# Single-block slot sums, VectorE log stores throughout, a first output chunk in halves, and a new order, in a one-core attention and soft-MoE kernel

## The chip, the cores and the metric

The kernel runs on one core of a Trainium2 chip, in float32. TensorE multiplies matrices into PSUM, VectorE (DVE), ScalarE (ACT) and GpSimd (POOL) do the rest, and SyncE (SP) issues the loads of the large tensors and every store. The metric is device time in microseconds of a whole execution. The kernel before was timed three times, and one more execution was profiled; all times below are from that execution, counted from the start of its span.

## The reference

Two stages follow each other. The first is an attention with 32 inducing points, the second a soft mixture of experts on its output. The names `q` and `c` below are used in this text again.

```python
def mab(q, kv):                       # twice: h = mab(I, x), then y = mab(x, h)
    s = scale * (q @ kv.T); s = s - s.max(-1)
    a = exp(s); a /= a.sum(-1) + 1e-9
    return a @ kv
logits = y @ phi                      # 45824 tokens, 32 slots
d = softmax over the tokens of logits # one maximum and one sum for each slot
slot_input = d.T @ y
slot_out = relu(slot_input @ w1[e]) @ w2[e]   # 8 experts, 4 slots each, F = 1024
c = softmax over the slots of logits
out = c @ slot_out
```

x is 4 batches of 11456 rows by 128. The slots' softmax runs over all tokens, so no row of the output exists before every row of x has been read and the experts are done.

## The kernel before, in words

**Chunks.** A batch is six chunks of 15 blocks of 128 rows, 24 chunks in all; a chunk is 128 x 1920 numbers, 960 KB. x is loaded as rows (`xn`) and, for chunks 6 to 23, a second time transposed (`xt`); TensorE transposes the first six.

**First pass** (for each batch). `s1p` = inducing points by x, maxima, exponentials, and `ha` = their product with x (L408); from the batch's sums come `hs`, `hts` and `bdg`.

**Second pass** (for each chunk). `s2p` = x by h (L332), a DVE transpose to `bt` (L579), maximum (L582), subtraction on POOL (L586), exponential on ACT, a TensorE transpose `tt` (L595), the product `lp` with `bdg` (L608), which gives logits and row sums at once, and the store of the logits into `l_all`. DVE stores them for 23 chunks (`ble`, L627, with the last block by ACT in `blf`); for chunk 17 (`BA`) ACT stores all 15 blocks one by one (`bla`, L648) and adds the logarithm's shift, so that POOL need not scale `bt` for it (`bml`, L652).

**Segments.** Three chunks make a segment, eight in all. Its slot maxima (`h0` or `blm`, `pt`, `pb`) are subtracted from the logits (`ds`, L727, on POOL or DVE), ACT takes the exponential (`de`, L730), and TensorE adds up the slot sums `u` (`c2`). For segments 3 to 6 (`C2P`) `c2` takes two blocks at a time: 64 x 64 products at L739, of which the halves on the diagonal are wanted, and four copies of 32 x 32 fetch them (L756). For the other four segments it takes one block at a time: fifteen 32 x 32 products at L745, and one copy (L758). A float32 product leaves two records in the trace.

**Experts.** `sit` joins the slot sums; `hpm` is the first layer (64 products for each of two halves, L902), `ga` the ReLU on ACT, `htm` a transpose, `gc` a DVE copy into `z2`, `so` the second layer (L931), `sos` its copy, `sr` the spread of it over all partitions (L941), and `srs` = `sr` times the reciprocal `rz` of the slots' sum (L944).

**Third pass and output.** The softmax over the slots (`soft`, L514 to L550, `ml` on POOL at L997, and a transpose back into `l_all` at L1000) can run for any chunk whose logits are there. Once `srs` exists, `po` (L1025) makes four products of 480 columns for each chunk, ACT and DVE copy them to `ot` (L1036), and SP stores `ot` (L1044). `SPLIT` gives how many of the four groups go in one store: chunk 1, which is stored first, goes in four stores.

**Order.** Nothing is scheduled at run time: `op` collects steps, and the string `ORDER` (two characters a step) says in which order they are written out. Each engine executes its own steps in that order, and waits with semaphores. PSUM has eight banks, taken in turn (`mm`). `fill` steps (L238) are products of 128 x 128 into a bank of their own that nothing reads; their operand is the tile that also holds `srs`, which is zero until L944 writes it.

Of the kernel before, what the change touches and what calls it, by code (L numbers as in the profile page):

```python
# [43 lines left out]
BA = [17]  # L44
C2P = [3, 4, 5, 6]
# [9 lines left out]
ORDER = (  # L55
    "000102030e0p0A0L0W3v3z0406080a0507090b0c0f0l0h0j0g0i0k0m0q0u0s0w0n0r0t0v0x0B0F0y0d0D0C0E0G0H0M0O0N0o0z17180P0S191a1f1g0Q1i1j0X11130Z0Y0I0R0T1012141l1h1k0J0U150K0V161b1c3D3H3L3P3w3A"
    "1d1m1e1o1phV1n3E1r1s1x1y1u1q1t1z3x3B1B1v3I1C1w3M3F1D3J1A3N1E1F1G1H3Q3R3S3T1K1X1L3U3V3W4b3Z4842451I2C2P2a1Y1M1Z3X401N1O202b211J2c3u3y3C3G3K3O683Y41321P434e2D2Q2E332R464f222d2e2f1Q23"
    "1R241S2F2S252g2T1T344g1U264447491V2G274ccj2h3536282i2H2j2k4a4d1W2Icr2l2n2J4h4icz2U29ck2mcscA4j2Kcl2L2o2p2M5f2q4n5s4k2Vct2rcBcmcucCcn2Nco2s2v2ycv2t2wcDcH4o4A6c6g6k6o6s676b6f6j6n6r8K"
    "4N694B4p4C6d2u2xcp4q4D2z2A4O6a6e5g4PcE5tcF5h37382W4l394r2X4s3a5i2Y4m2Z3bcq3c303d4t5j5u4Q2O5v4E4R5w2BcIcJ3f6h6p6l5F6i6t3g4u3h3i3j4v3k3n4F6m6q6u5G6v6w4wcw4S4G4T3l5k4H5l4I5H4zcx5I6x6y"
    "3m6z6C4U5x5y4V4xcKcP6A5m6D6B6E5J6F4J4W6I4X4K6G6J4Y4L4y5K6OcL6L3e4Z3q315z506R6H6K6McycQ6S51cX6P5L5McG5n5A525o5B6T3o5pcY4M5E5N5OcM5C6N6Q8L6UcR6V6W535D6X545P5Q3r5q70d5cS3p7d5556587q3s"  # L60
    "575b8M717e727f7r7S7T5S7s7U8O8S8W90948J8N8R8V8Z938T8i8P8Q737gcN8X5991855a8U8Y92745c5R7t7h7u5d7V7W5ecO956Y756Z5T7i7v763t7jcTcZ7796975U98997X787w5V7k7x868j9a878k799b9ed65r887l9h7y5W89"
    "8l9c9f7m9d9g7a7z7n7A7Y7p5X609k7o7b8a9i9lcUcV7B8b637Z9j9m7D8m9n809q9o9t8c8n7E9u5Y64d78o8d619r9p9sdd81cW7F8e9vd08fdl9w7c7Cde8h845Z7G9x8p8gd17H9y7I82df9z8q7J8r8s8t9E9S62a67K65ayd87LaM"
    "7M7N9Fdg9G9T9Ua7aza8aAaNaO9H7O9Vd99I7P839Wdhb07Qa966aa9J9A9X9KaBaC9YaPb19Bb2ab9LaQ9Macbrbsbtbubvbwbxbybz8u9Ndi9Ob3bB9Za0b4aD8v9PaEa18wa29Rad8xaRaFb5ae8ya3aSafaga5ahaj9Qa4aTaGaHbCaI"
# [86 lines left out]
def tile_kernel(ctx, tc, x0, xn, xt_d, ind_t, phi, w12, w3, consts, out):  # L150
# [417 lines left out]
    def second(n):  # L568
# [592 lines left out]
```

## Time and profile before

| | us |
|---|---|
| three timed executions | 217.75, 219.30, 220.89 |
| their median | 219.30 |
| the profiled execution, whole | 219.41 |
| span of its profile | 217.4 |
| TensorE busy | 193.3 (89%) |
| DVE, ACT, POOL busy | 163.3, 141.9, 124.4 |
| read and written | 49.84 MB and 23.59 MB |

The span is what lies between the first and the last instruction of the trace; 2.0 us of the profiled execution lie around it. Busy shares are means over very different stages, so a stage is read by the rows of its own stretch: which engine has no gap there, and what the last wait ends on.

### The profile page before, as it was taken

How to read it: one execution, taken by the hardware profiler on the slowest of the kernel's cores; microseconds unless marked ns; L12 is line 12 of the kernel's file. 1: busy time of each engine (PE TensorE's matmuls, PEld its weight loads, DVE VectorE, ACT ScalarE, POOL GpSimd, SP SyncE). 2: the span in 40 equal slices, each digit the busy share in tenths (PEclk: the TensorE clock that was granted, in tenths of full speed). 3: DMA queues.
4: the chain of work that ended last, by engine and by line, in shares of the span. 5: the costliest groups of instructions: out<-in, count | busy, mean ns of one | idle time of the engine just before them, and what ended most of it. 6: DMA issues, size and time to landing. Idle time of an engine off the chain costs nothing.

```text
span 217.4 us, 6563 instructions
## 1 busy us (share of the span) xinstructions
PE 193.3 (89%) x2614; PEld 131.8 (61%) x2614; DVE 163.3 (75%) x371; ACT 141.9 (65%) x395; POOL 124.4 (57%) x137
## 2 busy tenths in 40 slices
PE   7889999999989999999999999999999799775510
PEld 7559674597365897469985698798554345232200
DVE  0114576999999999999987899777968888856240
ACT  2578442975637994449979798724489998936030
POOL 0000000588986968986976699799846686570300
PEclk9999999999999999999999999999999996755585
DMA  6999999998899999999999930000099999999995
GB/s 217 383 425 417 413 417 413 417 417 325 259 397 418 424 414 414 403 414 417 416 417 413 420 154 3 2 8 3 19 400 415 404 427 411 427 410 425 413 392 206
DMA packets 12414, 73.86 MB, mean 340 GB/s; under 512 B 1632, under 2 KB 2272, under 8 KB 12384
## 3 DMA queue, kind: packets, MB, share of 16 engines
q1 hardware_dynamic: 11952, 73.27, 83.3%
q8 instruction: 21, 0.34, 0.6%
q10 hardware_dynamic: 432, 0.17, 0.3%
q14 instruction: 9, 0.07, 0.1%
HBM read 49.84 MB, written 23.59 MB: 338 GB/s over the span
## 4 chain that ended last, share of the span: by engine, by line
PE 70%; DVE 12%; DMA 4%; ACT 4%; issue 2%; POOL 2%; SPq 1%; POOLq 0%; DVEq 0%; ACTq 0%
PE po L1025 12%; PE ha L408 10%; PE s2p L332 9%; PE s1p L332 9%; PE lp L608 8%; PE tt L595 5%; DMA xn<-xn 4%; PE u L739 4%; PE tp L309 3%; DVE ot L1036 2%; DVE l_all L1000 2%; POOL ct L997 2%; PE so L931 2%; PE fill L238 2%; DVE cm L514 2%
## 5 line engine op out<-in xcount | busy, mean ns | idle before, releaser
L1025 PE MATMUL po<-l_all,srs 32*128 32x480 f32 x192 | 41.2, 744 | 9.1 <-DVE l_all L1000 8.5
L1036 ACT COPY ot<-po 128x480 f32<-128x480 f32 x65 | 32.8, 583 | 10.9 <-PE po L1025 10.9
L1025 PEld LDWEIGHTS po<-l_all,srs 32*128 32x128 f32 x192 | 18.8, 219 | 29.5 <-issue 12.3
L586 POOL TENSOR_TENSOR bt<-bt,bm 128x480 f32<-128x480 f32 x24 | 23.6, 995 | 13.8 <-DVE bm L582 12.1
L997 POOL TENSOR_TENSOR ct<-ct,cz 128x480 f32<-128x480 f32 x24 | 23.6, 995 | 13.4 <-DVE cz L550 13.4
L608 PE MATMUL lp<-bdg,a2t 128*128 128x132 f32 x192 | 25.4, 277 | 0.7 <-issue 0.7
L343 DVE TENSOR_SCALAR_CACHE_REDUCE s<-s1p 128x480 f32<-128x480 f32 (+1 forms) x24 | 15.0, 646 | 14.2 <-PE s1p L332 13.9
L727 POOL TENSOR_TENSOR d<-l_all,m_all 128x512 f32<-128x512 f32 x19 | 21.8, 1166 | 6.5 <-issue 3.5
L608 PEld LDWEIGHTS lp<-bdg,a2t 128*128 128x128 f32 x192 | 23.3, 190 | 1.6 <-issue 1.3
L1036 DVE COPY ot<-po 128x480 f32<-128x480 f32 x31 | 18.9, 638 | 6.2 <-PE po L1025 6.1
L652 POOL TENSOR_TENSOR bt<-bt,bz 128x480 f32<-128x480 f32 x23 | 22.6, 997 | 0.3 <-DVE cz L550 0.3
L523 POOL TENSOR_TENSOR ct<-l_all,cm 128x512 f32<-128x512 f32 x18 | 18.8, 1051 | 5.8 <-DVE l_all L1000 5.3
L389 ACT ACTIVATE s<-s,negm 128x480 f32<-128x480 f32 (+1 forms) x24 | 16.6, 694 | 6.2 <-DVE negm L374 6.2
L332 PE MATMUL s1p<-xt,it_sb 128*32 128x480 f32 x160 | 19.3, 570 | 0.7 <-ACT xt L317 0.7
L1000 DVE STREAM_TRANSPOSE l_all<-ct 128x480 f32<-128x480 f32 x24 | 15.6, 659 | 5.0 <-POOL ct L997 5.0
L408 PE MATMUL ha<-xn,e 128*32 128x128 f32 x570 | 19.0, 275 | 0.0
L332 PE MATMUL s2p<-xt,hts 128*32 128x480 f32 x160 | 18.9, 571 | 0.0
L345 POOL MEMSET s<- 128x16 f32 x4 | 0.4, 112 | 31.1 <-DVE e L392 30.8
L527 ACT ACTIVATE ct<-ct 128x480 f32<-128x480 f32 x24 | 14.6, 616 | 5.0 <-POOL ct L523 4.7
L589 ACT ACTIVATE bt<-bt 128x480 f32<-128x480 f32 x24 | 14.1, 610 | 4.9 <-POOL bt L586 4.8
L579 DVE STREAM_TRANSPOSE bt<-s2p 128x480 f32<-128x480 f32 x24 | 15.6, 665 | 2.1 <-PE s2p L332 1.1
L408 PEld LDWEIGHTS ha<-xn,e 128*32 128x32 f32 x570 | 16.1, 109 | 1.6 <-PE s2p L332 0.6
(142 smaller groups left out, 390.5 us busy)
## 6 DMA issues: line engine op xcount, KB each, us to landing
out<-ot SPq DMA_DIRECT2D x20, 960.0 KB, 7.9
xn<-xn SPq DMA_DIRECT2D x18, 960.0 KB, 12.6
xt<-xt SPq DMA_DIRECT2D x14, 960.0 KB, 14.7
w<-w SPq DMA_DIRECT2D x8, 960.0 KB, 14.8
l_all<-xn SPq DMA_DIRECT2D x5, 960.0 KB, 10.1
l_all<-xt SPq DMA_DIRECT2D x4, 960.0 KB, 6.8
out<-ot SPq DMA_DIRECT2D x6, 480.0 KB, 5.0
out<-ot SPq DMA_DIRECT2D x4, 240.0 KB, 2.3
```

The costliest lines, as they stand in the source:

```text
L332: nc.tensor.matmul(dst[32 * g : 32 * g + 32, :w], lhs, src, start=True, stop=True)
L389: nc.scalar.activation(t[:, :v], t[:, :v], AF.Exp, bias=T["negm", b, g], accum_out=z6[:, a : a + 1])
L408: nc.tensor.matmul(ha[32 * q : 32 * q + 32, :P], T["e1", a][:, j * S : (j + 1) * S], T["xn", a][:, j * P : (j + 1) * P], start=c == lo and ...
L523: nc.gpsimd.tensor_tensor(t.rearrange("p (a e s) -> p a e s", s=S, e=2), l_blocks(n), m, op=ALU.subtract)
L586: nc.gpsimd.tensor_tensor(t, t, T["bm", n][:, :nb].unsqueeze(2).broadcast_to(full), op=ALU.subtract)
L608: nc.tensor.matmul(pt[:, q * 4 * SZ : (q * 4 + m) * SZ], t[: m * S, q * P : (q + 1) * P], bdgs[b % 2].rearrange("p q s -> p (q s)")[: m * ...
L652: nc.gpsimd.tensor_tensor(t, t, T["bz", n][:, :nb].unsqueeze(2).broadcast_to(full), op=ALU.mult)
L727: e.tensor_tensor(t.rearrange(o, s=S, e=2), l_pairs(n), m, op=ALU.subtract)
L997: nc.gpsimd.tensor_tensor(t, t, T["cz", n][:, :nb].unsqueeze(2).broadcast_to([P, nb, S]), op=ALU.mult)
L1000: nc.vector.transpose(l_of(n), T[ck][:, :w])
L1025: nc.tensor.matmul(ptile("mm", ("po", 4 * n + g))[:, :w], T["srs",][q, :], l_of(n)[q, :], start=True, stop=True)
L1036: (nc.vector.tensor_copy if dve else nc.scalar.copy)(ot[:, g * w : (g + 1) * w], T["po", m][:, :w])
```

## The change

The change takes `BA` and `C2P` out, with the code that they switched on: all 24 chunks have their logits stored by `ble` and `blf` and their `bt` scaled by `bml`, and all eight segments sum their slots one block at a time, with one copy each. Without the logarithm the early load of ACT's function table goes too. In the experts `rz` is now applied by DVE in `ge`, on the way from `so` to `sos`, and `gs` becomes an ACT copy. Chunk 1 (`HEAD`) gets its four output products in halves of 240 columns, DVE and ACT copying two groups each, and is stored in four stores of other shapes. The `fill` steps go from 16 to 10. Costs in `op` calls are used by nothing at run time. `ORDER` is new throughout.

```diff
-BA = [17]
-C2P = [3, 4, 5, 6]
-SPLIT = {0: 4, 1: 1, 2: 4, 3: 2, 22: 2, 23: 4, 10: 2, 21: 4, 5: 4}
+SPLIT = {0: 4, 2: 4, 3: 2, 22: 2, 23: 4, 10: 2, 21: 4, 5: 4}
+HEAD = 1
-NF = 16
+NF = 10
 ORDER = (
-    "000102030e0p0A0L0W3v3z0406080a0507090b0c0f0l0h0j0g0i0k0m0q0u0s0w0n0r0t0v0x0B0F0y0d0D0C0E0G0H0M0O0N0o0z17180P0S191a1f1g0Q1i1j0X11130Z0Y0I0R0T1012141l1h1k0J0U150K0V161b1c3D3H3L3P3w3A"
...
+    "000102030e0p0A0L0W3v3z3D0406080507090a0b0c0f0l0h0j0g0i0k0m0q0w0u0s0n0r0t0v0x0B0D0y0d0o0z17180F0M0H0Q190C0E0N0G0O0S1a1f1i0P0I1g1j0X0Z13110Y100R0T12141l1h1k0J0U153H3L3P3u3y3A3w0K0V16"
...
-    if BA:
-        nc.scalar.preload_act_table_set("natural_log_exp_and_others")
...
-        if n in BA:
-            op("ACT", 0.2 + (0.17 if valid(n) < w else 0), ("bln", n), bln, [("bz", n)], [("bl", n)])
-            op("ACT", 0.1 + 0.19 * nb, ("bla", n), bla, [("lp", n), ("bz", n), ("bl", n), *need], [("l", n), ("lx", n), *first], [(x[0], x) for x in first])
-        else:
...
-                for j in [0, 2, *range(nb - 1, 3, -2 * nb), *range(4, nb - 1, 2)] if k in C2P else ():
-                    r, h = min(2, nb - j), 64 * (j // 2 % 2)
-                    nc.tensor.matmul(
-                        u[h : h + r * S, : r * S], a2[:, j * S : (j + r) * S], d[:, j // 2, :r], start=i == 0 and j < 4, stop=i == seg - 1 and nb - 6 < j < nb - 1,
-                    )
-                for j in range(nb) if k not in C2P else ():
+                for j in range(nb):
                     q = slice(32 * (j % 4), 32 * (j % 4) + 32)
                     c = slice(j * S, j * S + S)
                     nc.tensor.matmul(u[q, :S], a2[:, c], d[:, j // 2, j % 2], start=i == 0 and j < 4, stop=i == seg - 1 and j >= nb - 4)
...
-                for q in range(4) if k in C2P else ():
-                    r = slice(32 * q, 32 * q + 32)
-                    nc.scalar.copy(us_all[r, k * S : (k + 1) * S], T["u", k][r, q % 2 * S : (q % 2 + 1) * S])
-                if k not in C2P:
-                    nc.scalar.copy(us_all[:, k * S : (k + 1) * S], T["u", k][:, :S])
+                nc.scalar.copy(us_all[:, k * S : (k + 1) * S], T["u", k][:, :S])
...
         def ge():
-            nc.vector.tensor_copy(stile("h", ("sos",), P, 1), T["so",][:, :P])
+            nc.vector.tensor_scalar_mul(stile("h", ("sos",), P, 1), T["so",][:, :P], T["rz", "l"])
...
         def gs():
-            nc.vector.tensor_scalar_mul(T["srs",], T["sr",][:, :P], T["rz", "l"])
+            nc.scalar.copy(T["srs",], T["sr",][:, :P])
...
+        cuts = [0, w // 2, w] if n == HEAD else [0, w]
+        parts = list(zip(cuts, cuts[1:]))
...
+                    nc.tensor.matmul(ptile("mm", ("po", n, g, h))[:, : hi - lo], T["srs",][q, :], l_of(n)[q, lo:hi], start=True, stop=True)
...
+                if n == HEAD:
+                    dve = g % 2 == 1
...
+        todo = [(0, 1, 0, w // 2), (1, 3, 0, w // 2), (3, 4, 0, w), (0, 3, w // 2, w)] if n == HEAD else [(g, g + step, 0, w) for g in range(0, 4, step)]
```

The order moves work at many places; three bear on what follows. All three are TensorE's.

The first is the end of the second pass, where the last segment's maxima go through `pt` and `pb`. `u_2268` (before) and `u_2313` (after) are the sums of segment 6, `hb` and `ufp` small products for the experts. Before:

```order
L238 MATMUL fill_2256<-srs 128x128
L696 MATMUL pt_2258<-cst,tm_2198 32x128 x3
L739 MATMUL u_2268<-d_2246,bt_1978 64x64 x2
L739 MATMUL u_2268<-d_2246,bt_1978 32x32
L739 MATMUL u_2268<-d_2246,bt_1978 64x64 x5
L703 MATMUL pb_2277<-cst,mc_2265 128x32
L739 MATMUL u_2268<-d_2248,bt_1984 64x64 x2
L739 MATMUL u_2268<-d_2248,bt_1984 32x32
L739 MATMUL u_2268<-d_2248,bt_1984 64x64 x5
```

And with the change:

```order
L235 MATMUL fill_2299<-srs 128x128
L675 MATMUL pt_2301<-cst,tm_2219 32x128 x3
L719 MATMUL u_2313<-d_2281,bt_1939 32x32 x15
L479 MATMUL hb_2329<-hs_1858,cst 128x128
L682 MATMUL pb_2331<-cst,mc_2311 128x32
L719 MATMUL u_2313<-d_2283,bt_1954 32x32 x15
```

Between `pt` and `pb` stood eight products of a pair sum; now fifteen single ones and `hb`, which came earlier before.

The second is the turn from the experts' first layer (`hpm`) to the second (`so`). Before:

```order
L902 MATMUL hpm_2453<-w_2077,ma 32x128 x8
L902 MATMUL hpm_2453<-w_2079,ma 32x128 x2
L915 MATMUL htm_2488<-cst,ma 128x128
L238 MATMUL fill_2496<-srs 128x128
L915 MATMUL htm_2498<-cst,ma 128x128
L931 MATMUL so<-w_2079,ma 32x128 x6
```

And with the change:

```order
L872 MATMUL hpm_2517<-w_2084,ma 32x128 x2
L885 MATMUL htm_2543<-cst,ma 128x128
L856 MATMUL zpp<-ones,vr 128x1
L872 MATMUL hpm_2517<-w_2084,ma 32x128 x6
L872 MATMUL hpm_2517<-w_2086,ma 32x128 x2
L901 MATMUL so<-w_2086,ma 32x128 x6
L901 MATMUL so<-w_2088,ma 32x128 x7
L901 MATMUL so<-w_2090,ma 32x128 x8
L901 MATMUL so<-w_2092,ma 32x128 x3
L885 MATMUL htm_2593<-cst,ma 128x128
L901 MATMUL so<-w_2092,ma 32x128 x4
```

The first half's transpose now stands inside the second half of `hpm`, and the second half's transpose inside the first half of `so`.

The third is the end of the experts and the first output products. Before:

```order
L931 MATMUL so<-w_2087,mb 32x128 x4
L886 MATMUL zpp<-ones,vr 128x1
L238 MATMUL fill_2593<-srs 128x128
L941 MATMUL sr<-sos,cst 128x128
L238 MATMUL fill_2598<-srs 128x128
L238 MATMUL fill_2600<-srs 128x128
L1025 MATMUL po_2603<-l_all,srs 128x480
```

And with the change:

```order
L901 MATMUL so<-w_2094,mb 32x128 x4
L911 MATMUL sr<-sos,cst 128x128
L1000 MATMUL po_0_0_2662<-l_all,srs 128x240
L1000 MATMUL po_1_0_2664<-l_all,srs 128x240
L1000 MATMUL po_2_0_2666<-l_all,srs 128x240
L1000 MATMUL po_3_0_2668<-l_all,srs 128x240
L1000 MATMUL po_0_1_2674<-l_all,srs 128x240
```

`zpp` has moved ahead, the three fills are gone, and so are five more that stood between the second and the third chunk's `po`. The two fills right ahead of `hpm` stay, and eight stand earlier.

## Rows read from the trace of the kernel before

**Rows 1.** Windows: stretch, length, busy PE, PEld, DVE, ACT, POOL, clock, DMA share, GB/s.

```profile
110.00:126.00 16.00, 16.00 (x210) 10.44 (x202) 13.12 (x25) 13.19 (x45) 10.66 (x11) 1.00 1.01 414
126.00:131.00 5.00, 5.00 (x46) 4.85 (x45) 4.91 (x13) 4.76 (x18) 5.00 (x6) 1.00 0.24 95
131.00:144.00 13.00, 12.83 (x235) 10.91 (x234) 10.35 (x28) 9.37 (x33) 11.27 (x14) 1.00 0.01 3
...
160.00:175.00 15.00, 13.73 (x79) 6.29 (x72) 13.04 (x27) 14.79 (x35) 9.63 (x11) 1.00 1.02 412
...
190.00:205.00 15.00, 8.44 (x32) 4.33 (x36) 8.05 (x17) 5.77 (x13) 6.59 (x8) 0.50 1.01 418
```

**Rows 2.** Timeline of SP, the first and the last stores: start us, us, operation.

```profile
156.50 0.82 SPq L1044 DMA_DIRECT2D out<-ot  x2
...
208.60 0.33 SPq L1044 DMA_DIRECT2D out<-ot  x1
...
210.62 0.42 SPq L1044 DMA_DIRECT2D out<-ot  x1
```

**Rows 3.** The chain that ended last: start us, us, engine, tile, line, records.

```profile
110.87 0.94 PE u L739 x16
...
136.93 1.01 PE u L739 x16
...
141.95 0.82 PE u L745 x60
...
153.68 0.36 DVE srs L944
154.08 0.71 PE fill L238 x4
154.79 1.82 PE po L1025 x16
156.62 2.25 PE fill L238 x10
...
203.66 3.67 PE po L1025 x16
```

**Rows 4.** Timeline of DVE, 118 to 153 us: idle time ahead in brackets, with what ended it.

```profile
118.05 0.68 DVE L579 STREAM_TRANSPOSE bt<-s2p 128x480 f32<-128x480 f32 x1 [0.51 <-PE u L739]
119.81 0.68 DVE L579 STREAM_TRANSPOSE bt<-s2p 128x480 f32<-128x480 f32 x1 [1.08 <-PE s2p L332]
...
152.82 0.28 DVE L938 COPY sos<-so 128x128 f32<-128x128 f32 x1
```

**Rows 5.** Timeline of ACT, four places.

```profile
4.16 0.29 ACT L230 COPY bdg<-cst 128x4 f32<-128x4 f32 x2 [2.14 <-DMA cst<-consts]
...
114.59 4.16 ACT L648 ACTIVATE l_all<-lp,bl,bz 128x32 f32<-128x32 f32 x15
...
140.04 0.74 ACT L756 COPY us_all<-u 32x32 f32<-32x32 f32 x4 [0.17 <-PE u L739]
...
155.91 2.87 ACT L1036 COPY ot<-po 128x480 f32<-128x480 f32 x6 [1.74 <-PE po L1025]
```

**Rows 6.** Timeline of PE, the experts' two layers.

```profile
144.01 3.70 PE L902 MATMUL hpm<-w,ma 128*32 128x128 f32 x128
...
148.88 1.95 PE L931 MATMUL so<-w,ma 128*32 128x128 f32 x64 [0.45 <-DVE ma L920]
150.66 1.93 PE L931 MATMUL so<-w,mb 128*32 128x128 f32 x64
```

**Rows 7.** Groups by line and form over the span: count, busy us, mean ns, idle before.

```profile
L1036 ACT COPY ot<-po 128x480 f32<-128x480 f32 x65 | 32.8, 583 | 10.9 <-PE po L1025 10.9
...
L652 POOL TENSOR_TENSOR bt<-bt,bz 128x480 f32<-128x480 f32 x23 | 22.6, 997 | 0.3 <-DVE cz L550 0.3
...
L627 DVE TENSOR_TENSOR l_all<-lp,bz 128x448 f32<-128x448 f32 x23 | 13.6, 604 | 0.3
...
L473 ACT COPY ht<-htp 128x128 f32<-128x128 f32 x4 | 1.1, 263 | 0.0
```

More of the change, by code (lines that the diff above doesn't have):

```diff
@@ L69 @@
+    "hFfjfqhGhwfrfshyfefthEhvhjhdhAhzfkflhxfuhnfvhHhIhMhohJhKfmfnhLhOhVhZhNhWhPhShXhQhYhRi0hUhphBhT"
 )
@@ L1019, in output @@
         w = width(n)
-        def mm():
-            btile("x", ("ot", n))
-            for g in range(4):
-                q = slice(32 * g, 32 * g + 32)
-                nc.tensor.matmul(ptile("mm", ("po", 4 * n + g))[:, :w], T["srs",][q, :], l_of(n)[q, :], start=True, stop=True)
-        po = [("po", 4 * n + g) for g in range(4)]
-        i = op("PE", 1.0, ("po", n), mm, [("srs",), ("l", n)], po, [("mm", k) for k in po] + [("x", ("ot", n))], ni=16)
-        plan.uses(("ot", n), i)
-        for g in range(4):
-            m = 4 * n + g
-            dve = g == 2 and n in OD or g == 1 and n in OD2
-            def ev(m=m, g=g, dve=dve):
-                ot = T["ot", n]
-                (nc.vector.tensor_copy if dve else nc.scalar.copy)(ot[:, g * w : (g + 1) * w], T["po", m][:, :w])
-            i = op("DVE" if dve else "ACT", dv(w) if dve else ac(w), ("oe", n, g), ev, [("po", m)], [("otg", m)])
-            plan.uses(("ot", n), i)
@@ L1041, in st, with mm, ev @@
-        def st(lo, hi):
+        cuts = [0, w // 2, w] if n == HEAD else [0, w]
+        parts = list(zip(cuts, cuts[1:]))
+        for h, (lo, hi) in enumerate(parts):
+            def mm(h=h, lo=lo, hi=hi):
+                if not h:
+                    btile("x", ("ot", n))
+                for g in range(4):
+                    q = slice(32 * g, 32 * g + 32)
+                    nc.tensor.matmul(ptile("mm", ("po", n, g, h))[:, : hi - lo], T["srs",][q, :], l_of(n)[q, lo:hi], start=True, stop=True)
+            po = [("po", n, g, h) for g in range(4)]
+            i = op("PE", 0.2 + (hi - lo) / 600, ("po", n, h) if h else ("po", n), mm, [("srs",), ("l", n)], po, [("mm", k) for k in po] + ([] if h else [("x", ("ot", n))]), ni=16)
+            plan.uses(("ot", n), i)
+            for g in range(4):
+                dve = g == 2 and n in OD or g == 1 and n in OD2
+                if n == HEAD:
+                    dve = g % 2 == 1
+                def ev(g=g, h=h, lo=lo, hi=hi, dve=dve):
+                    (nc.vector.tensor_copy if dve else nc.scalar.copy)(T["ot", n][:, g * w + lo : g * w + hi], T["po", n, g, h][:, : hi - lo])
+                i = op("DVE" if dve else "ACT", dv(hi - lo) if dve else ac(hi - lo), ("oe", n, g, h) if n == HEAD else ("oe", n, g), ev, [("po", n, g, h)], [("otg", n, g, h)])
+                plan.uses(("ot", n), i)
@@ L1052, in output @@
+        for g0, g1, lo, hi in todo:
+            src = [("otg", n, g, h) for g in range(g0, g1) for h, (x, y) in enumerate(parts) if x < hi and lo < y]
+            i = op("DMA", 2.50 * (g1 - g0) * (hi - lo) / 2048, ("st", n, g0, lo) if n == HEAD else ("st", n, g0), st(slice(g0, g1), lo, hi), src, [("out", n, g0, lo)])
             plan.uses(("ot", n), i)
```

59 lines of the change are left out of this document (23 added, 36 removed).

## The prediction

> **What bounds the kernel now.** I read the end first. From its first store at 156.50 us [rows 2] the kernel writes 23.59 MB, and the windows show 412 and 418 GB/s there [rows 1]: 23.59 / 0.415 = 56.8 us of pure transfer, in a remainder of 217.4 - 156.5 = 60.9 us. So the tail is bound by the stores, and a whole execution ends 60.9 us after the first store, plus the 2.0 us outside the span. What can be won is what brings the first store forward, as long as the stores are then fed.
>
> Next the windows ahead of it [rows 1]. From 110 to 126 us TensorE has no gap (16.00 of 16), while DVE (13.12), ACT (13.19) and POOL (10.66) do; DVE's gaps end on TensorE [rows 4]. From 126 to 131 us all four are busy 4.76 to 5.00 of 5: no one of them sets the pace alone. From 131 to 144 us TensorE is busy 12.83 of 13, but with the zero products among it, and the other three have gaps: a chain of short steps, each waiting for the last. Then come the experts [rows 6], the spread of their result [rows 3], and the first copy to the output at 155.91 [rows 5].
>
> The sum is made against the profiled execution's own 219.41 us, which lies 0.1 us from the median of the timed ones (219.30); I carry the difference over unchanged.
>
> **The change part by part.**
>
> *Slot sums.* A pair sum takes 16 records, 0.94 us on the chain; 60 records of single blocks, two chunks, take 0.82 us, so 0.41 us a chunk [rows 3]. Twelve chunks change: 12 x 0.53 = 6.4 us less of TensorE. Here a rule speaks against the change. TensorEngine Tiling in the Trainium skill, section Instruction Overhead, gives every product some 60 cycles whatever its width, and warns against splitting along a dimension that is already small; as an estimate from that page at 2.4 GHz, 30 records would take 0.75 us against 0.43 us for 16 of 64 columns, so the six chunks below would make the first term +1.9 in place of -2.2, and the sum -1.1. The trace disagrees with it: 0.82 us for 60 records is 14 ns each, and the pair products have 59 ns each.
>
> Six of the twelve chunks (segments 3 and 4) lie in the stretch from 110 to 126 us where TensorE has no gap: 6 x 0.53 = 3.2 us. DVE can follow only as far as its own gaps go, 16 - 13.12 = 2.9 us, and it gets the store of chunk 17 in addition, 0.60 us [rows 7]: 2.3 us. ACT loses 4.16 us there [rows 5], and POOL gets one multiplication of 1.00 us [rows 7] where it has 5.3 us free. I take **-2.2**; the ends are 0 (DVE's work falls in another order and no gap closes) and -3.2 (all of it), and DVE's gaps are the nearer bound.
>
> *131 to 144 us.* Ahead of `pb`, the spread of the last segment's maxima, stands one pair sum, 1.01 us [rows 3]; the order now has one single sum and `hb` there, 0.41 and about a third of a us: -0.3. ACT's four copies of segment 6, 0.74 us at 140.04 [rows 5], stand ahead of the last exponentials; one copy takes their place: 0.74 x 3/4 = -0.55. The other pair sums of segments 5 and 6, five at 0.53, are partly hidden behind POOL and DVE: a fifth of 2.6 counted, -0.55. Together **-1.4**, between -0.3 (the copies alone, half hidden) and -2.4. Chunk 17's new work costs nothing here, it lies before; the early table load costs nothing either, since ACT's first work waits 2.14 us for the constants [rows 5].
>
> *Turn between the layers.* `hpm` ends at 144.01 + 3.70 = 147.7 and `so` starts at 148.88 after waiting for DVE [rows 6]: 1.2 us. With the first transpose inside `hpm` and the second inside `so` this wait is covered by products; the transposes and `zpp` themselves, some 0.55 us of issue, now lie inside. **-0.6**, between 0 (the ReLU or the DVE copy stands behind other steps on its engine) and -1.2.
>
> *From `so` to the first product.* The two fills read `srs`, so they start only when it is written, and take 0.71 us ahead of `po` [rows 3]: all of that goes. `sos` (0.28 us) gets a scale; `srs` goes from DVE's 0.36 us to an ACT copy of that shape, 0.26 us [rows 3, 4, 7]; these two cancel. **-0.7**, between -0.4 and -1.0 according to whether DVE and ACT are free then.
>
> *Halves.* Two chunks of `po` take 1.82 us [rows 3], so four half products come 0.45 us sooner; a half copy lies between 0.26 us (128 columns) and 0.58 us (480) [rows 7], near 0.36: 0.2 us sooner. The first store comes 0.65 us earlier. But eight half products hold all eight banks, eight copies take 8 x 0.36 = 2.9 us instead of 4 x 0.58 = 2.3 us on the two engines, and the second chunk waits for banks: the first chunk lasts only 0.983 / 0.412 = 2.4 us on the queues. Against it, the ten fill records that stood 2.25 us between the second and the third chunk are gone [rows 3]. I take **-0.3**, between +0.6 (a hole in the stores) and -0.65.
>
> Sum: -2.2 - 1.4 - 0.6 - 0.7 - 0.3 = -5.2, so 219.4 - 5.2 = **214.2 us**. All good ends give 219.4 - 8.4 = 211.0, all bad ones 219.3.
>
> **The rivals.**
>
> *DVE and POOL hold the second pass.* For it: between 126 and 131 us POOL is busy 5.00 of 5 and DVE 4.91 [rows 1], and the change gives them chunk 17's store and multiplication; what TensorE saves earlier is then spent waiting here. Against it: both have gaps in the 16 us before. The first term goes, and half of the second: 219.4 - 0.7 - 0.6 - 0.7 - 0.3 = 217.1 us. Chance 0.18.
>
> *The stores run dry.* From 160 to 175 us ACT is busy 14.79 of 15 and DVE 13.04 [rows 1], while the queues run full; and the stores at 208.60 and 210.62 [rows 2] are issued so late that little was waiting ahead of them: what is left at 208.60, two and a half chunks of 2.4 us, ends near 214.6. The third pass uses the gaps ahead of the experts; if these gaps are cut by 5 us, about half of that work moves into the tail and the last stores come later after the first. Against it: from 190 to 205 us every engine has half of its time free. Half of the gain is given back: 219.4 - 2.6 = 216.8 us. Chance 0.14.
>
> *TensorE's clock falls before the experts.* This is the one that ends slower. The granted clock is 1.00 up to 175 us with TensorE nearly always busy (13.73 of 15), and 0.50, the level of 1.2 GHz, from 190 us, with 8.44 of 15 [rows 1]. At that level 16 `po` records take 3.67 us instead of 1.82 [rows 3]. The change takes 6.4 us of products out of 110 to 144 us, and leaves TensorE waiting for DVE. If the clock falls there and is low when `hpm` starts, the two layers, 3.70 and 3.7 us [rows 6], double: 214.2 + 7.4 + 0.5 for the first products = 222.1 us. It decides only if it falls ahead of `hpm`; later the stores hide it, 3.67 / 2 = 1.8 us a chunk against 2.4 us on the queues. Against it: 34 us of that stretch hold 33.8 busy us; without 6.4 of them and 3.6 us shorter, nine tenths stay busy, and eight fills stand ahead of the experts. Chance 0.05.
>
> *A single product costs what a pair product does.* If width did not matter in the new places, a record would take 0.94 / 16 = 59 ns, and thirty 1.76 us: six chunks in TensorE's stretch, 6 x 0.82 = +4.9 us, against -1.6 from the end: 222.7 us. The 60 records at 14 ns speak against it. Chance 0.01. It is what the rule of the Trainium skill, TensorEngine Tiling, section Instruction Overhead, would come to here.
>
> **How the numbers follow.** The forecast keeps 0.62; its own range is 212.4 to 216.2. To hold 8 in 10 the range must reach over the first two rivals and part of the good ends: 211.2 to 218.8. About 2% (4.4 us, below 215.0 us) is what can be told from no change. Some three quarters of the forecast's chance lie below 215.0, 0.47, with 0.02 from the better parts of the rivals: 0.49 faster. The rest of the forecast, most of the first two rivals, and the weaker parts of the slow ones are within 2%: 0.46. Slower by over 2%, above 223.8 us, would take the fallen clock with something more: 0.05.
>
> **What would show it.** First store near 151 us in the new trace, and then 60 to 61 us to the end. Each single sum at 0.41 us, with DVE's waits for TensorE between 110 and 126 us gone. `so` starting within 0.2 us of `hpm`, `po` within 0.1 us of `srs`. The granted clock at 1.00 until the first stores. It is wrong if the experts start less than 2 us earlier than 144.0, if the first store is early and the GB/s of a later stretch fall under 400, or if the clock reads 0.50 ahead of 150 us.

## The result, and the profile after

| | before | changed |
|---|---|---|
| median of 20 executions each, us | 218.71 | 217.23 |
| lowest to highest, us | 217.74 to 220.89 | 214.78 to 221.22 |
| profiled execution, us | 219.41 | 217.6 |
| its span, us | 217.4 | 215.5 |

The ratio is 0.991 (95% interval 0.988 to 0.994): faster by 0.9%, some 2.0 us, where 5.2 us were forecast. All ratios in this document leave out the executions that lie over 1.5% above the fastest of their kernel (6 of the 20 changed ones); medians are over all of them.

The windows of the changed kernel, with the columns of [rows 1], and the group of its instruction queue (packets, MB, share of the DMA engines; before it had 21 packets):

```profile
100.00:110.00 10.00, 8.47 (x187) 7.51 (x189) 7.69 (x21) 7.88 (x27) 8.48 (x9) 1.00 1.02 416
110.00:126.00 16.00, 15.18 (x319) 10.72 (x311) 14.95 (x28) 10.83 (x35) 13.13 (x14) 1.00 1.01 411
126.00:131.00 5.00, 4.89 (x43) 4.39 (x42) 4.98 (x13) 4.35 (x17) 5.00 (x6) 1.00 0.24 96
131.00:144.00 13.00, 12.05 (x352) 10.32 (x354) 12.27 (x30) 7.11 (x22) 12.81 (x18) 0.90 0.02 4
144.00:154.00 10.00, 9.15 (x250) 7.63 (x240) 7.51 (x21) 3.52 (x11) 7.59 (x9) 0.95 0.01 2
160.00:175.00 15.00, 14.10 (x66) 7.14 (x63) 12.92 (x28) 14.35 (x35) 11.73 (x13) 0.91 1.02 416
190.00:205.00 15.00, 8.52 (x32) 3.30 (x28) 8.21 (x16) 7.01 (x16) 2.24 (x3) 0.61 1.01 416
```

```profile
q8 instruction: 22, 0.36, 0.7%
```

DVE did take the work from 110 to 126 us (14.95 against 13.12). New are the first row, with TensorE idle for 1.5 of 10 us, and the clock of 0.90 and 0.95 around the experts; before, two of these windows read:

```profile
100.00:110.00 10.00, 10.00 (x204) 9.38 (x206) 9.84 (x23) 9.95 (x32) 9.37 (x10) 1.00 1.02 417
144.00:154.00 10.00, 9.19 (x267) 8.18 (x266) 8.25 (x22) 3.49 (x9) 9.25 (x13) 1.00 0.02 4
```

TensorE's timeline shows the first; its waits from 58 to 131 us (total, times, longest) name what ended it:

```profile
103.30 1.81 PE L405 MATMUL ha<-xn,e 128*32 128x128 f32 x55
106.63 0.30 PE L405 MATMUL ha<-xn,e 128*32 128x128 f32 x1 [1.53 <-issue]
106.86 0.38 PE L453 MATMUL hp<-zt,cst 128*128 128x1 f32 x2
```

```profile
PE ha L405 <- issue: 1.5, 1, 1.5
PE lp L605 <- ACT d L709: 0.6, 1, 0.6
```

In the middle of `ha`, whose operands were all there, TensorE waits for nothing that the profile shows. The second wait it puts down to ACT's exponential `d`, which `lp` does not read; this text counts it with the first, by its place, for reasons given under The stops. The timeline through the experts, which answers to [rows 6] and to the end of [rows 3], then ACT's row of `srs`, then SP's row of the stores:

```profile
141.22 0.95 PE L235 MATMUL fill<-srs 128*128 128x128 f32 x4
142.10 4.61 PE L872 MATMUL hpm<-w,ma 128*32 128x128 f32 x112
146.64 0.33 PE L885 MATMUL htm<-cst,ma 128*128 128x128 f32 x1
...
147.02 0.64 PE L872 MATMUL hpm<-w,ma 128*32 128x128 f32 x16
147.48 1.49 PE L901 MATMUL so<-w,ma 128*32 128x128 f32 x48
...
152.04 0.49 PE L911 MATMUL sr<-sos,cst 128*128 128x128 f32 x2 [0.47 <-DVE sos L908]
152.89 1.09 PE L1000 MATMUL po<-l_all,srs 32*128 32x240 f32 x16 [0.35 <-ACT srs L914]
```

```profile
152.57 0.27 ACT L914 COPY srs<-sr 128x128 f32<-128x128 f32 x1 [0.74 <-PE sr L911]
```

```profile
154.19 52.85 SPq L1020 DMA_DIRECT2D out<-ot  x30
```

`so` follows `hpm` without a wait and `po` follows `srs`, as the change meant. But 112 records of `hpm` take 4.61 us where 128 took 3.70 [rows 6]: a window over 141.5 to 144.9 us reads a granted clock of 0.50. The first store comes at 154.19, 2.3 us sooner [rows 2], and the span ends 61.3 us later (60.9 before).

### The profile page after: what moved, and what is told of

It is laid out like the page before. It is cut to its first block, busy times and chain, and to the rows that moved or that the text cites. A ratio compares the mean times of both kernels' runs of the same rounds, so it can differ in the third digit from the quotient of the medians.

```text
span 215.5 us, 6873 instructions
## 1 busy us (share of the span) xinstructions
PE 188.7 (88%) x2778; PEld 129.7 (60%) x2778; DVE 162.6 (75%) x375; ACT 135.5 (63%) x368; POOL 125.5 (58%) x138
## 4 chain that ended last, share of the span: by engine, by line
PE 59%; DMA 10%; DVE 9%; POOL 7%; issue 4%; ACT 3%; SPq 1%; DVEq 0%; ACTq 0%; POOLq 0%
PE po L1000 10%; PE s1p L329 9%; PE ha L405 9%; PE s2p L329 7%; DMA w<-w 6%; PE lp L605 6%; DMA xn<-xn 4%; DVE ot L1011 4%; PE tt L592 4%; PE tp L306 3%; POOL d L706 3%; PE hpm L872 2%; POOL bt L583 2%; PE u L719 2%; DVE l_all L970 2%
## 5 line engine op out<-in xcount | busy, mean ns | idle before, releaser
L1000 PE MATMUL po<-l_all,srs 32*128 32x480 f32 (+1 forms) x200 | 43.6, 746 | 3.8 <-DVE l_all L970 1.8
L1000 PEld LDWEIGHTS po<-l_all,srs 32*128 32x128 f32 x200 | 22.0, 229 | 24.4 <-ACT ot L1011 10.5
L1011 ACT COPY ot<-po 128x480 f32<-128x480 f32 (+1 forms) x65 | 31.8, 576 | 7.4 <-PE po L1000 7.1
L635 POOL TENSOR_TENSOR bt<-bt,bz 128x480 f32<-128x480 f32 x24 | 23.5, 1003 | 2.8 <-DVE bz L617 1.9
L1011 DVE COPY ot<-po 128x480 f32<-128x480 f32 (+1 forms) x35 | 20.2, 602 | 3.3 <-PE po L1000 3.3
L405 PE MATMUL ha<-xn,e 128*32 128x128 f32 x570 | 19.6, 275 | 1.6 <-issue 1.5
L329 PE MATMUL s1p<-xt,it_sb 128*32 128x480 f32 x160 | 19.8, 571 | 0.8 <-ACT xt L314 0.7
L329 PE MATMUL s2p<-xt,hts 128*32 128x480 f32 x160 | 19.6, 571 | 0.0
L709 ACT ACTIVATE d<-d 128x512 f32<-128x512 f32 x24 | 14.9, 633 | 5.9 <-POOL d L706 5.0
L389 DVE STREAM_TRANSPOSE e<-s 128x480 f32<-128x480 f32 x24 | 15.6, 657 | 1.9 <-ACT s L386 1.7
```

The lines of the kernel that those rows point to most:

```text
L329: nc.tensor.matmul(dst[32 * g : 32 * g + 32, :w], lhs, src, start=True, stop=True)
L405: nc.tensor.matmul(ha[32 * q : 32 * q + 32, :P], T["e1", a][:, j * S : (j + 1) * S], T["xn", a][:, j * P : (j + 1) * P], start=c == lo and ...
L635: nc.gpsimd.tensor_tensor(t, t, T["bz", n][:, :nb].unsqueeze(2).broadcast_to(full), op=ALU.mult)
L1000: nc.tensor.matmul(ptile("mm", ("po", n, g, h))[:, : hi - lo], T["srs",][q, :], l_of(n)[q, lo:hi], start=True, stop=True)
L1011: (nc.vector.tensor_copy if dve else nc.scalar.copy)(T["ot", n][:, g * w + lo : g * w + hi], T["po", n, g, h][:, : hi - lo])
```

## The experiments

Terms used below: the *second-pass stretch* runs from the broadcast `pb` of the first segment to that of segment 5; a *stop* is a gap of TensorE behind its 193rd record, or a multiple of 256 records after that one, that ends within 1.6 us after the end of a packet of the instruction queue. Every record of TensorE counts here: weight loads, products and waits for semaphores. A stop is measured from the start of the record ahead of it to the start of the next if that is over 0.3 us, so it holds that record's own time too (1.80 us where the timeline has 1.53 us idle). All of this is worked out from the traces.

### One part undone, or one part alone

**u_pairs**: the changed kernel with this part of its diff reversed.

```
+C2P = [3, 4, 5, 6]
...
+                for j in [0, 2, *range(nb - 1, 3, -2 * nb), *range(4, nb - 1, 2)] if k in C2P else ():
```

> The changed kernel, its order kept, with the pair products (and the four copies behind them) back in segments 3 to 6; the single products are undone alone. Theory 1, the single products pay little because the second pass is held elsewhere (GpSimd's chain of multiplies and subtractions, and 1.5 us at 105 us in which TensorE waits for nothing the profile shows): the pair sums lie on TensorE where it has gaps now, so the time rises by only 0.5 to 1.2 us, to 217.8 to 218.4 (0.995 of before); the stall near 105 us stays and the first expert layer still takes 4.6 us at a clock below 1.00. Rival, the single products themselves brought both losses (they run through TensorE's instructions faster and leave it thinner work ahead of the experts): with pairs the gap near 105 us shrinks below 0.5 us, the clock is 1.00 from 131 to 146 us, the first expert layer takes 3.7 us, and the time is within 0.5 us of the changed kernel (216.7 to 217.7, 0.992).

222.31 us, 1.014 (1.009 to 1.019). Far above both expectations. The clock stayed at 1.00 and `hpm` was fast, as the rival said, but it started at 147.48, 5.4 us later than in the changed kernel; the stop stayed too (1.61 us, at the same place):

```profile
110.00:126.00 16.00, 16.00 (x221) 10.23 (x214) 12.73 (x25) 9.16 (x32) 11.73 (x12) 1.00 1.01 414
...
147.48 3.26 PE L882 MATMUL hpm<-w,ma 128*32 128x128 f32 x112
```

**u_ba**: chunk 17's logits by ScalarE again, in the changed kernel (`BA = [17]`, with a step that does nothing in the place of GpSimd's multiply).

> The changed kernel, its order kept, with the logits of chunk 17 written by ScalarE again in 15 activations behind a logarithm (and so no GpSimd multiply of that chunk). If GpSimd's chain ahead of 126 us holds the second pass (its multiply of chunk 17 stands ahead of the first subtraction of the last batch), one multiply of 1.0 us less there ends the last slot maximum up to 1.0 us sooner, and the time falls to 216.2 to 216.8 (0.987). If ScalarE holds it there (a product waits 0.65 us on an exponential now), 15 activations of some 0.2 us in place of one of 0.28 us make it later: 218 to 219.5 (1.000), with TensorE waiting on ScalarE between 112 and 118 us.

220.95 us, 1.007 (1.003 to 1.011): the second branch, and more. TensorE is busy for 12.29 of the 16 us from 110, against 15.18, and between 50 and 131 us its longest wait is one for ScalarE:

```profile
PE tt L595 <- ACT bt L589: 3.2, 1, 3.2
```

**order_only**: the new order with every part undone.

> The changed kernel's order of work with every other part of the change undone: pair products and their four copies, chunk 17's logits by ScalarE, the division behind the second turn by VectorE, the first stored chunk whole and in quarters. (The fills at the end stay out, since the new order holds none there.) If the new order alone carries the gain: 217.0 to 217.6 (0.992). If the parts carry it and the order only makes room for them, this one gives back the pair sums (0.5 to 1.2), the turn (0.4) and the halves (0.3): 218.3 to 219.3 (1.000).

229.86 us, 1.047 (1.042 to 1.052). Both sides missed: with the same parts as before, the new order alone costs 11 us. So undoing a part in it can charge that part with a misfit, and u_ba does not price its part (bsi_noba, below, finds nothing of it in the old order). For u_pairs the charge lies in the later half: its second-pass stretch less its stop is 74.4 us, 3.6 above the changed kernel's 70.8, near the 3.4 that the same exchange is worth in the old order (the table at the end); the rest comes behind the stretch, where the way to `hpm` takes 16.92 us against 14.21.

**b_singles**: the reverse test, one part alone in the order of before.

```
-C2P = [3, 4, 5, 6]
+C2P = []
```

> The kernel before, in its own order, with nothing changed but the slot sums of segments 3 to 6, single products and one copy each. By my sum for the stretch ahead of the experts, with the order not made for it: the pair sums' 0.3 to 1.0 us come off the chain between the last slot maximum and the experts, 217.7 to 218.4 (0.997). If single products cost TensorE its clock ahead of the experts, the first expert layer goes from 3.70 to above 4.3 us with a clock below 1.00 between 135 and 150 us, and the time is 218.5 to 219.5 (1.002). If the chip charged a single product what it charges a pair product, 120 more at 59 ns in place of 14 would make it 5 us slower.

217.46 us, 0.985 (0.979 to 0.991; of its six executions the ratio counts three). The single products alone, in the old order, gain as much as the whole change by the medians; a record that cost the same at any width, the fourth rival, is ruled out. In the profiled execution, the longest of the six (219.44 us), the clock falls ahead of the experts and `hpm` takes 5.70 us (the windows, then TensorE's row):

```profile
131.00:142.00 11.00, 9.75 (x301) 8.43 (x301) 8.27 (x21) 6.44 (x20) 9.48 (x12) 0.78 0.01 4
142.00:154.00 12.00, 12.00 (x272) 10.84 (x271) 8.54 (x21) 3.02 (x9) 9.04 (x13) 0.78 0.01 3
```

```profile
143.21 5.70 PE L902 MATMUL hpm<-w,ma 128*32 128x128 f32 x128
```

### The clock ahead of the experts

**a_hold** and **bs_hold** move fills to where TensorE waits, the first in the changed kernel, the second in b_singles. In the order's method, with `sums` the last segment's three slot sums:

```
+        move(fills[8], sums[0])
+        move(fills[9], sums[1])
+        move(fills[7], sums[2])
+        move(fills[6], sums[2])
```

```
+        for i in fills[11:14]:
+            move(i, at["h3", NSEG - 1])
+        move(fills[14], sums[0])
+        move(fills[15], sums[1])
+        move(fills[5], sums[2])
```

> The changed kernel with the same ten fills, four of them at other places of TensorE's queue: the two right ahead of the first expert layer and two of the six behind segment 6 now stand ahead of the three slot sums of the last segment, where TensorE waits 0.65 us on ScalarE. In the changed kernel's trace the granted clock is 0.50 from 141.5 to 144.9 us, and the first expert layer takes 4.61 us up to its first turn. Theory (thin work and gaps on TensorE ahead of the experts let the clock fall, and that costs 1.35 us from the layer's start to the first store: 12.09 us here, 10.74 us with the pair products, whose clock stays at 1.00): with the gaps filled the clock is 1.00 from 131 to 150 us, the layer's first part takes below 3.4 us, from its start to the first store 10.7 us, and the time is 215.2 to 216.2 (0.985). Rival, it is the single products' own light work and not the gaps: the clock falls all the same, and the time stays within 0.5 us of 217.2, or rises by the 0.2 to 0.5 us for which a fill stands ahead of a slot sum.

> The kernel before with single products and its own order, and six of its sixteen fills at other places: the five that stood behind the first chunk's stores, and one ahead of the first expert layer, now stand ahead of the last broadcast of the slot maximum and of the last segment's three slot sums. With single products alone the trace shows the clock at 0.50 from 137.1 to 147.3 us, ten microseconds in which the chain runs through TensorE. Theory: with the gap of 0.8 us filled the clock holds, the first expert layer takes 3.70 us instead of 5.70 and starts about 1.5 us earlier than 143.2, and the time falls by 2 to 3.5 us below that of single products alone, to 214 to 215.5 (0.980). Rival, single products are too light work for the clock whatever fills the gaps: 0.50 again for at least 3.4 us between 135 and 148, and the time is 217 to 218.

a_hold 217.43 us, 0.992 (0.989 to 0.995); bs_hold 217.28 us, 0.993 (0.990 to 0.996). Both traces have the clock at 1.00 and the fast layer; a_hold goes from the start of `hpm` to `po` in 9.44 us against 10.79. For a_hold:

```profile
142.00:154.00 12.00, 10.63 (x292) 9.08 (x286) 11.08 (x28) 3.94 (x12) 10.70 (x13) 1.00 0.01 3
...
143.17 3.27 PE L885 MATMUL hpm<-w,ma 128*32 128x128 f32 x112 [0.34 <-DVE ma L876]
```

No gain in time was measured from either; the trace of a_hold has another stop, of 0.84 us behind record 449 at 25 us, ahead of all this. In the old order the clock read 1.00 with the fills moved (bs_hold, bs_best and bs_pace) and 0.78 and 0.79 without (b_singles and bsi_pace), but also 1.00 without in bsi_noba, below, which has single products, the old order and every fill in its old place. In the new order it also held in a_pad and a_pace, whose fills stand where they did. So the fall is not in every execution, and that the fills hold the clock is not shown in either order.

**bs_best**: bs_hold with the end of the change in the old order.

```
+        q = [i for i in q if i not in fills[9:11]]
+        dve = [i for i in q if self.ops[i][0] == "DVE"]
+        move(at["gc", 0], dve[dve.index(at["gc", 0]) - 1])
...
-            nc.vector.tensor_scalar_mul(T["srs",], T["sr",][:, :P], T["rz", "l"])
+            nc.scalar.mul(T["srs",], T["sr",][:, :P], T["rz", "l"])
```

> The same kernel with the changed one's cure for the stretch behind the second expert layer as well, without its order: the division behind the second turn by ScalarE (a scaled copy) instead of VectorE, no fills between it and the first stored product, and the copy of the first turn of the hidden layer one step earlier in VectorE's queue. By the changed kernel's trace (from the first layer's start to the first store 10.74 us at full clock against 12.49 before) these are worth 0.6 for the two fills, 0.1 for ScalarE and up to 0.45 for the copy: 212.9 to 214.3 (0.975), faster than both kernels. If the stretch is held by VectorE instead (the sum `sos` and the division's input), it is within 0.3 us of the version without them.

216.46 us, 0.989 (0.986 to 0.993): from `hpm` to `po` 10.20 us against bs_hold's 10.82; the time missed the range. The stops sum to 3.83 us in this trace (bs_hold 4.83).

### The stops

**a_pad** shifts TensorE's instructions against the pieces in which they come.

```
-        warm_into(ptile("mm", ("warm0",)), 8)
+        warm_into(ptile("mm", ("warm0",)), 5)
+        for _ in range(38):
+            nc.tensor.matmul(T["warm0"][:32, :32], wz[:, :32], wz[:, :32], start=True, stop=True)
```

> The changed kernel with 32 records more... of TensorE at its start: three full warm-up products fewer, 38 products of 32 by 32 more, 64 instructions more in all and 0.2 us less work. In all four kernels with the new order TensorE stops for 1.3 to 1.8 us behind the same instruction, number 3265 of its records, 35 instructions after a 16 KB packet on the instruction queue starts; the next such packet's place is 256 instructions on, and there too it stops (0.9 us). Theory, TensorE waits for its own instructions, which come in pieces of 256 and late while the loads fill the DMA engines: the stop moves with the pieces and not with the operation, so behind record 3265 again (64 instructions earlier in the program), longer or shorter or gone, and not in the middle of the last `ha` where it stands now. Time 216.5 to 218 either way. Rival, the stop belongs to that operation (its operands, a queue of its own): it stands at the same product of `ha`, now record 3329.

218.0 us, 0.993 (0.989 to 0.997). The edit adds 140 records to the trace ahead of the stop (the expectation counts 64). The stop moved with the pieces: it is behind record 3265 again, now a different product, and shorter; nothing stops near 3405, where the old product went. There are new ones, the longest behind 3009 (0.80 us) and 4033 (1.30 us), all 256 apart or multiples of it:

| kernel | behind record | at, us | gap, us | from the packet's end to the next record |
|---|---|---|---|---|
| before | 1729 | 62.3 | 0.95 | 1.46 |
| changed | 3265 | 104.8 | 1.80 | 1.28 |
| changed | 3521 | 112.9 | 0.92 | 1.40 |
| a_pad | 3265 | 104.4 | 0.82 | 1.23 |
| a_pad | 4033 | 122.4 | 1.30 | 1.54 |
| b_singles | 1729 | 62.4 | 1.28 | 1.48 |
| b_singles | 3777 | 117.5 | 1.87 | 1.47 |

For the changed kernel's second row the profile names ACT's exponential, which ended at 113.55 us, 0.29 us ahead of `lp`. `lp` reads nothing of it, in bs_hold and bs_best the wait behind record 3521 is one on "issue", and in a_light, below, it is gone, so it is counted as a stop.

**a_pace, b_pace, bsi_pace, bs_pace**: changed, before, b_singles and bs_best with the weight loads spread by small transfers that wait for VectorE.

```
+        nc.sync.dma_start(late[:1, i : i + 1], src[:1, :1])
         nc.sync.dma_start(parts(wt[i]), w12[i].rearrange("h p w -> p h w"))
...
+            while pace and pace[0] in done and len(wt) > len(PACE) - len(pace):
+                t, n = pace.pop(0)
+                issue(len(PACE) - len(pace) - 1, T["bm" if t == "bmx" else "bz", n])
```

> The changed kernel, all of its work and order kept, with the nine loads of the expert weights spread over the second pass: each is issued behind a 4-byte transfer that waits for a block maximum or a reciprocal of the second pass (from about 98 us on, every 4 us, to 132), so that the DMA engines are not full from 104 to 126 us. TensorE's instructions come in packets of 16 KB; in all ten kernels profiled so far it stops ahead of 131 us only where such a packet is late (behind record 193 and every 256th from there), and goes on 1.2 to 1.5 us after the packet's end: 0.94 us in all before, 2.33 after. Theory (the single products use up instructions faster than the full DMA engines bring them, and that took back a part of their gain): with free DMA engines the stops behind records 3265 and 3521 (1.80 and 0.92 us) vanish, the last slot maximum of the second pass ends 0.9 to 2 us sooner than 126.2 us, and the time is 215.2 to 216.4 (0.986). Rival, GpSimd's or VectorE's chain sets the end of the second pass whatever TensorE does: the stops vanish and the time stays at 217.2 +- 0.5.

> Control: the kernel before with its weight loads spread in the same way. Its only stop ahead of the experts in that stretch is 0.38 us behind record 3521. Theory: -0.1 to -0.4 us, 218.3 to 218.8 (0.999); nothing else in the kernel waits for a load there. If the loads slow more than the instructions (contention of any other kind), it gains as much as the changed one, above 1 us.

> The kernel before with the single products alone, and its weight loads spread. In its own trace with single products three stops lie in that stretch or shortly ahead (0.34 behind 2753, 0.41 behind 3521, 1.87 us behind 3777); the last two should vanish. Theory: 1.5 to 2.2 us below single products without the spreading, 215.0 to 216.5 (0.985), and against the control the single products are then worth 2.3 to 3.5 us, near the 3.6 that the prediction had for them. Rival: the stops lay beside other engines' work, and it stays within 0.5 us of 217.4.

> Single products, fills that hold the clock, ScalarE's division and no fills ahead of the first stored product, in the order of the kernel before, now with the weight loads spread. Without the spreading it took 216.5 us, with stops of 1.22 and 1.60 us behind records 3521 and 3777. Theory: those vanish, 213.7 to 215.2 (0.980), faster than both kernels. Rival: within 0.5 us of 216.5.

a_pace 216.52 us, 0.992 (0.988 to 0.996); b_pace 218.91, 0.9995 (0.996 to 1.003); bsi_pace 217.4, 0.989 (0.983 to 0.994); bs_pace 215.46, 0.985 (0.980 to 0.989). The control b_pace gained nothing (0.1 us above its range). The stop behind 3777, where the DMA share fell to about 0.8, is gone in bsi_pace and bs_pace, but most of it comes back as a wait for ScalarE a little later; in bsi_pace:

```profile
119.28 0.45 PE L746 MATMUL u<-d,bt 128*32 128x32 f32 x30 [0.86 <-ACT d L731]
```

The one behind 3265 in a_pace stayed (1.87 us), since the loads of `x` still keep the DMA engines full up to 112 us there. The times of a_pace and bsi_pace missed; bs_pace missed its range by 0.3 us.

**a_light, b_light, bsi_light** take the DMA load away there: a_pace, b_pace and bsi_pace with the pacing begun later and the last loads of `x` cut.

```
+        return 8 if a >= 18 and tag_of("xn", a) == "x" else JM
...
+                    m = P * part_of(a)
+                    nc.sync.dma_start(parts(t)[:, :, :m], xn[a - 1].rearrange("h p w -> p h w")[:, :, :m])
```

> The changed kernel with its weight loads spread (from about 108 us on) and with the last loads of x cut: of the chunks of the last batch that have a buffer of their own only 8 of 15 blocks are loaded, and the products and transposes use these 8 again for the rest, so that part of the input is left out and the work of every engine stays the same. The DMA engines should have free time from about 97 us on. Theory (the stop at 105 us, behind record 3265, is on TensorE's path and took back most of what the new order gained in the second pass): the stop vanishes, the last `ha` ends 1.2 to 1.8 us sooner than 110.9 us, the broadcast of segment 5's maximum comes 1 to 1.8 us sooner than 127.9, and the time is 214.5 to 216 (0.982). Rival, VectorE and GpSimd hold the second pass in this order: `ha` ends sooner, and the broadcast and the time stay (127.9 +- 0.4; 216.5 to 217.2).

> Control: the kernel before with the same loads cut and the weight loads spread alike. It has one stop of 0.38 us in that stretch and TensorE is busy throughout: 218.3 to 219.0, within 0.3% of before. If it gains over 1 us, the loads hold the kernel in some other way than through instructions, and the gain of the changed one must be read against it.

> Single products alone in the order of before, with the same loads cut and the weight loads spread. Its stops behind 3521 and 3777 should be gone; the one of 1.28 us behind 1729, at 62 us, stays. Theory: against the control the single products are worth 2.5 to 3.5 us (215.2 to 216.4, 0.985), the last `ha` to the broadcast of segment 5 takes 14.3 to 14.8 us against 17.3 in the control. Rival: within 0.5 us of 217.4, the stops beside other work.

a_light 216.07 us, 0.985 (0.981 to 0.990); b_light 218.8, 0.9996 (0.997 to 1.003); bsi_light 218.48, 0.994 (0.990 to 0.997). All three have no stop from 100 to 131 us. The window 104 to 108 us, in the changed kernel and then in a_light, and a_light's `ha` of that place, 60 records in one run:

```profile
104.00:108.00 4.00, 2.47 (x50) 2.08 (x39) 1.78 (x7) 2.06 (x6) 2.99 (x3) 1.00 1.02 413
```

```profile
104.00:108.00 4.00, 4.00 (x81) 3.71 (x80) 3.59 (x11) 3.73 (x11) 3.89 (x5) 1.00 0.01 4
```

```profile
104.39 1.95 PE L410 MATMUL ha<-xn,e 128*32 128x128 f32 x60
```

The DMA share goes from 1.02 to 0.01, and TensorE from 2.47 to 4.00 busy us. Broadcasts of the first segment and of segment 5 in the changed kernel and in a_light:

```profile
54.39 0.40 PE L682 MATMUL pb<-cst,mc 32*128 32x32 f32 x2
...
127.89 0.40 PE L682 MATMUL pb<-cst,mc 32*128 32x32 f32 x2
```

```profile
55.07 0.40 PE L687 MATMUL pb<-cst,mc 32*128 32x32 f32 x2
...
126.37 0.40 PE L687 MATMUL pb<-cst,mc 32*128 32x32 f32 x2
```

The stretch is 73.50 us in the first and 71.30 in the second; the control went from 73.96 to 73.45, with its one stop of 0.95 us gone. a_light met its expectation for the broadcast, while its last `ha` ended only 0.6 us sooner; its time of 216.07 lies just above the range. The loads that it moved keep the DMA engines busy later (share 0.99 from 130 to 134 us), and there is a new stop there, of 0.88 us behind record 4545 at 137.2 us; the clock fell to 0.50 from 137.8 to 144.6 us. Together they ate what had been won. bsi_light missed: its profiled execution has such a stop too (1.47 us behind 4545) and the clock at 0.78 through the experts (`hpm` 5.90 us), and its second-pass stretch (71.06) is the shortest of all.

**bsi_noba**: b_singles with chunk 17's logits by VectorE (`ble` in the place of ScalarE's logarithm, `blf` and `bml` in that of its 15 activations).

> Single products in the order of before, and chunk 17's logits as in the change: one VectorE multiply in the place of ScalarE's logarithm, ScalarE's single copy and GpSimd's multiply in the place of its 15 activations. If this part of the change is worth something by itself (2.6 us less of ScalarE, which TensorE waits for in the second pass), the time falls to 216.0 to 216.9 (0.988). If it is a loss (GpSimd has 0.95 us more ahead of its subtractions of the last batch, VectorE 0.58), the stretch from the last `ha` to the broadcast of segment 5 grows from 15.15 to 15.7 us or more and the time rises to 217.8 to 218.6 (0.996).

217.12 us, 0.989 (0.983 to 0.995): neither branch. By itself this part changes nothing that was measured.

## Why the prediction was wrong

The forecast's steps, in the profiled executions (us; the third column is from traces without the disturbance):

| step | forecast | changed | without it |
|---|---|---|---|
| slot sums: up to the broadcast of segment 5 | -2.2 | -0.24 (128.13 to 127.89; -0.46 by the stretch) | -2.15 (a_light against b_light, 71.30 - 73.45) |
| from there to `hpm` | -1.4 | -1.67 (15.88 to 14.21) | -1.6 (a_hold) |
| turn and fills, `hpm` to `po` | -0.6 - 0.7 | +0.07 (10.71 to 10.79) | -1.27 (9.44 in a_hold, a_pad, a_pace) |
| halves, `po` to the first store | -0.3 | -0.48 (1.78 to 1.30) | |
| first store to the end | 0 | +0.40 (60.93 to 61.33) | |
| sum | -5.2 | -1.9 | |

The step that failed is the first, *slot sums*: -0.24 us in place of -2.2. The working had DVE's gaps as the nearer bound, and DVE closed them. What it left out, and so put at nothing, is the time in which TensorE has no instructions: 0.95 us before, 2.72 us with the change. The trace shows the instructions in packets of 16 KB on a queue of their own; the change takes TensorE from 2614 products to 2778, each with a weight load, and with its waits from 5326 records to 5653 (20.8 and 22.1 pieces of 256, for 21 and 22 packets), and packs 30 product records of 0.45 us where 16 of 0.94 us stood. While the loads keep the DMA engines full, in the changed kernel between 80 and 124 us, a packet starts 2.6 to 5.9 us after TensorE has gone into the piece ahead of it; from 127 to 135 us, with a DMA share under 0.1, 0.4 to 0.8 us. TensorE is through a piece in 4.7 to 8.4 us, so at the dense places it arrives first. That the stops lie on the path is shown by the second-pass stretch less its stops:

| kernels | stretch | stops | difference |
|---|---|---|---|
| before, b_pace, b_light | 73.96, 74.25, 73.45 | 0.95, 1.25, 0 | 73.0, 73.0, 73.5 |
| changed, a_hold, a_pad, a_pace, a_light | 73.50, 73.54, 74.12, 73.40, 71.30 | 2.72, 2.46, 3.79, 2.38, 0 | 70.8, 71.1, 70.3, 71.0, 71.3 |
| b_singles, bs_hold, bs_best, bsi_noba | 72.19, 73.46, 72.42, 73.08 | 3.56, 4.83, 3.83, 4.47 | 68.6, 68.6, 68.6, 68.6 |
| bsi_pace, bs_pace, bsi_light | 71.61, 72.20, 71.06 | 1.65, 2.24, 1.00 | 70.0, 70.0, 70.1 |

Within a group the difference varies far less than the stops: most of their time is paid, in the new order some three quarters to nine tenths of it. The exception is the stop behind 3777: without it (the last row against the one above) the stretch is only 0.2 to 0.6 us shorter for a stop of 1.6 to 1.9 us, as the wait for ScalarE takes its place. Without stops the first term measures -2.15 us against the forecast -2.2. That it agrees so closely is in part luck: in the old order the single products are worth 3.4 us without stops (b_light against bsi_light), more than the 2.9 us of DVE's gaps that the working took as a bound, and the new order, which this term did not price, takes 1.2 us back. The table also says that the new order is longer in this stretch than the old one with the same single products, by 1.2 us without stops (a_light against bsi_light) and by 2.2 in the changed kernel against b_singles; it has some of that back behind the stretch, at the turn and the fills (`hpm` to `po` 9.44 us at full clock against 10.71 in bsi_noba). Why the new order is longer there was not tested.

The second miss is the rival *TensorE's clock falls before the experts*, held at 0.05. It came in part: not for both layers but for 3.4 us, and it cost 1.35 us from `hpm` to `po`, just what turn and fills gave (9.44 at full clock). The argument against it, nine tenths of that stretch still busy, does not decide it: from 137 to 140 us TensorE was busy 2.35 of 3, but at the same place of a_pad and a_pace 2.36 of 3, and there the clock held. What set off the fall is open.

The rival *DVE and POOL hold the second pass* names nearly the measured time, 217.1, but not the cause: with the stops gone the stretch is 2.2 us shorter at the same work of both. *The stores run dry* did not happen: 416 GB/s through the tail. The halves and the chain behind the second pass came out as sized, and a single sum at 0.45 us for 30 records. By its own list the prediction is wrong on the experts' start (142.10, 1.9 us sooner and not 2) and on the clock.

The rule of the Trainium skill, TensorEngine Tiling, section Instruction Overhead, some 60 cycles for a product of any width, does not hold here as the prediction used it, as time for each product in a row: 30 records in 0.45 us are 15 ns each, where the estimate had 25, and b_singles is faster. What one product takes alone is not shown: single records last some 0.2 us in the trace, with modelled ends, and overlap. A price for many small products there is all the same, but it is paid in whole stops.

The fastest kernel is bs_pace, the old order with single products, moved fills, the end of the change and spread weight loads: 215.46 us, 0.985 (0.980 to 0.989), against 0.991 (0.988 to 0.994) for the change. The intervals touch, so that it beats the change is likely, not shown.

## What to carry to other kernels

When a change replaces few long products by many short ones, count the instructions as well as the time, and look in the trace for waits on "issue" at equal distances of records: where transfers are full, TensorE can run out of instructions, and each time cost up to 2.1 us here. An order of work that was fitted to a set of changes is a change of its own; price a part alone in the old order too, since undoing it in the new one can charge it with a misfit (+5.1 us by the medians for the pair products here, against 0.3 to 1.5 us gained by single ones in the old order, bsi_light against its control and b_singles, stops and clock falls included).

## What the runs showed of the hardware

- TensorE's waits on "issue" of over half a us in the second pass come behind records 193 + 256 k, waits for semaphores counted (3265 in the changed kernel and, 140 records earlier in its work, in a_pad), and end 1.2 to 1.6 us after the end of a 16 KB packet on the instruction queue. With the DMA share at 0.01 instead of 1.02 at the same place (a_light), the stop of 1.8 us was gone.
- Their lengths change from execution to execution: the one behind record 1729 took 1.28, 2.13 and 1.01 us in the profiled executions of b_singles, bs_hold and bs_best, which are alike up to there.
- Ahead of the experts the granted clock fell to 0.50 for 3.4 us (changed), 6.8 us (a_light, bsi_pace) or 10.2 us (b_singles, bsi_light), each time behind gaps of TensorE, and it stayed at 1.00 in others with gaps as large: 2.36 busy us of 3 in a_pad and a_pace ahead of `hpm` against 2.35 in the changed kernel.
